# Reordering the first convolution steps and the second group's layer norm in a fused H3 + gated-MLP kernel

## The chip, the cores and the metric

The kernel runs on one core of one Trainium2 chip. The time is the device time of one execution in microseconds; the figure for a version is the median of its runs. A separate execution was recorded by the hardware profiler; its rows are what the durations below come from. In the profile PE is TensorE's matmul row, PEld its weight loads, DVE is VectorE, ACT is ScalarE, POOL is GpSimd and SP is SyncE, whose own instructions (SPq) issue nearly all DMAs of this kernel.

## The reference, cut to what matters

The input `x` (`A_q`) has 2048 rows of 640. Its rows are layer-normed to `xn`, and the output is `x` plus two branches of `xn`:

```python
xn = layernorm(x)                                   # per row, 640 wide
kv = shift_conv(k, shift_k) * v                     # 4 taps along the sequence
y  = irfft(rfft(kv, 4096) * rfft(ssm_k, 4096))[:2048]   # causal convolution by FFT
A  = xn * (y + kv * ssm_D)
B  = (sigmoid(xn @ w_gate) * (xn @ w_up)) @ w_down  # 640 -> 1728 -> 640
out = x + A + B
```

All data are bf16, with float32 accumulation.

## The kernel before, in words

**Layout.** Row `16p + b` of the sequence lies on partition `p`, block `b`; there are 16 blocks, handled as four groups of four (`g` or `t` in the code). The MLP works on one group (512 rows) at a time. The convolution works on five chunks of 128 channels (`c`), for all 2048 rows, as a discrete Fourier transform in stages: a first stage of matmuls against a cosine and sine table `S1t`, a write to DRAM and a read back in another arrangement, a second stage, the product with the kernel's transform, and two inverse stages.

**MLP.** For a group, each of 13 columns of 128 takes a gate product and an up product (`product`, L281, five matmuls of 512 columns into one PSUM tile), ScalarE's sigmoid (L290) and VectorE's multiplication into `hT` (L296); a last, narrower one is done in one go (L302, L308, L311). Then come eight down tiles (L325), each of two half-tiles of seven matmuls, evicted by VectorE, which adds them onto `x` (L330). All these PSUM tiles rotate through four buffers (`psG`). The products read `xnT`, the transposed `xn` of the group; it has one buffer. For the first group it is made by TensorE; for groups 1 to 3 by four DMA transposes (`xn_turn`, L260), one a block, called turns here.

**Layer norm of a group** (`ln_norms`, L210 and L214: statistics of a block; `ln_pow`, L222: GpSimd's power −1/2; `ln_xn`, L227: VectorE's subtraction and multiplication). For the second group alone (`g == 1`), two of its four blocks are normalised by ScalarE (`ln_xn_act`, L239), for which GpSimd first works out a bias (`ln_shift`, L233 and L234). Its input block of `x` is loaded by L135 in the middle of the table loads.

**Convolution.** VectorE makes `kv` (L358 to L367, sixteen instructions a chunk) and transposes the filter (L344); GpSimd adds `ssm_D` to it (L338). A first-stage step (`st1_mm`, L384 and L386) is eight matmuls into one of two PSUM buffers (`psC`), evicted by ScalarE (`st1_ev`, L242). A chunk has eight such steps; steps 0 to 3 read the first half of `S1t`, steps 4 to 7 the second. Two steps make a tile of 512 KB, which SyncE writes to DRAM (`wr1`, L402), four writes a chunk; `rd2` (L419) reads it back.

**Order.** Nothing is reordered by a scheduler. Every function call is a step of a chain named by a letter, and the string `ORDER` says from which chain the next step is taken; each engine runs its instructions in that order. The letters that matter here: `g` a product or a down half-tile on PE; `s` sigmoid; `u` VectorE's eviction of a product or down tile; `a` a first-stage step and `A` its eviction; `w` a write of it; `l` a block's statistics or its normalisation on VectorE; `P` the power on GpSimd; `x` the normalisation on ScalarE; `e` a turn; `k` one of `kv`'s instructions; `H` the filter's transposition, `D` the addition on GpSimd; `K` loads of `k`, `T` of the taps, `n` of later groups of `x`.

**SyncE's queue.** All DMAs but a few at the start are issued by SyncE, in the string's order. An instruction that waits there holds all those behind it. The build gives the queue eight semaphores in turn, so that a DMA also waits until the one eight places before it has landed.

The change lies in the second row of `ORDER`, where group 0's down tiles, the first-stage steps of chunk 0 (and the first ones of chunk 1) and the second group's layer norm meet, just ahead of the second group's products.

Of the kernel before, what the change touches and what calls it, by code (L numbers as in the profile page):

```python
# [11 lines left out]
F32 = mybir.dt.float32  # L12
U16 = mybir.dt.uint16
ACT = mybir.ActivationFunctionType
ALU = mybir.AluOpType
# [4 lines left out]
P = 128  # L20
# [37 lines left out]
def kernel(  # L58
# [14 lines left out]
    nc = tc.nc  # L73
# [15 lines left out]
    cv = ctx.enter_context(tc.tile_pool(name="cv", bufs=1))  # L89
# [16 lines left out]
    x = res.tile([P, NB, DM], BF16, name="x")  # L106
    xn = res.tile([P, NB, DM], BF16, name="xn")
# [93 lines left out]
    lns = [dict() for _ in range(4)]  # L201
# [22 lines left out]
    def ln_xn(g, i):  # L224
# [1 line left out]
        d = lns[g]  # L226
        nc.vector.tensor_scalar(xn[:, b, :], x[:, b, :], d["mv"][:, i, 0:1], d["rstd"][:, i:i + 1],  # L227
                                op0=ALU.subtract, op1=ALU.mult)

    def ln_shift(g, lo):  # L230
        d = lns[g]
        d["nb"] = cv.tile([P, 4], F32, name="nb")
        nc.gpsimd.tensor_tensor(d["nb"][:, lo:4], d["mv"][:, lo:4, 0], d["rstd"][:, lo:4], ALU.mult)  # L233
        nc.gpsimd.tensor_scalar(d["nb"][:, lo:4], d["nb"][:, lo:4], -1.0, None, op0=ALU.mult)  # L234

    def ln_xn_act(g, i):
        b = 4 * g + i
        d = lns[g]
        nc.scalar.activation(xn[:, b, :], x[:, b, :], ACT.Identity, bias=d["nb"][:, i:i + 1], scale=d["rstd"][:, i:i + 1])  # L239

    def act_copy(out, in_):
        nc.scalar.copy(out=out, in_=in_)  # L242
# [310 lines left out]
        up_ev(0, fc)  # L553


    chains = {k: [] for k in "ABCDHKPRTVWZabcdeghklmnopqrstuwx"}

    def step(k, fn, *args):
        chains[k].append((fn, args))
# [87 lines left out]
                    step(k, *a)  # L647

    for g in range(1, 4):
        for i in range(4):  # L650
            step("l", ln_norms, g, i)
        step("P", ln_pow, g, 0, 4)
        if g == 1:
            step("P", ln_shift, g, 2)
        for i in range(4):
            if g == 1 and i >= 2:
                step("x", ln_xn_act, g, i)
            else:
                step("l", ln_xn, g, i)
        for i in range(4):  # L660
            step("e", xn_turn, g, i)

# [8 lines left out]

    ORDER = """
    mmmZmmmmmmmmmTmmmmmmmggsguggsggsuukkgggssukkggukksukkkgsgukkgggsgukkkggsgsukkguHstggguHDmmmsukkkkggg
    ulagluaAKglulaAwAaAgPPukalAlkkHDkweegakkAxxeeTggakgggaAaAgKwaukgukAHukggAukkwsgggnustagukKKgghakAsul
    rwAsakggluglsaksAugHggkAVrubkkkBlswKBukgggaTVsgpkusukawgDkHPlngAaAaskgAKwAkukgskpbgtkBsllBugauAkgagp
    sAaguswVpakAguhkHHAgrgDkwcgVklguCkkraeCagAgkAbuBkuBkkggKgkbBKpggBaeualwukkggeIuurlTklAehrgwtVbBBggag
    kAagppswuAagkuaKswrgpAAkaHAskWgHupDgakuVsAggswucglJukkgkrCsbgpBugaBaAgAWkkgsbspugPkrBgwpgsRnFkukgprc
# [40 lines left out]
```

## Time and profile before

| | |
|---|---|
| Median of 3 runs | 234.88 us (233.32 to 235.01) |
| Profiled execution: device time | 236.44 us |
| Profiled execution: span from first to last instruction | 234.7 us |
| Mean granted TensorE clock | 0.999 |
| PE busy, idle | 227.9 us (97%), 6.8 us |
| DVE busy | 203.4 us (87%) |
| ACT busy | 123.4 us (53%) |
| DMA queue 1 (SyncE's and ScalarE's) | 56.03 MB, 93.4% of 16 engines' span |

The profiled execution's device time is 1.7 us more than its span, and 1.56 us more than the median of the runs. In the profile's rows a matmul's duration overlaps with the next one's; how fast PE goes is read from the distance of their starts. Rows of SPq are the issuing of a DMA and not its transfer; the trace also has the time at which most DMAs landed.

### The profile page before, as it was taken

What the parts mean: (1) busy time and instruction counts of PE and PEld (TensorE: products, weight loads), DVE (VectorE), ACT (ScalarE), POOL (GpSimd) and SP (SyncE); (2) the same over time, 40 slices, a digit from 0 to 9 for tenths busy, and PEclk for the clock granted to TensorE, in tenths of its full rate; (3) what the DMA queues carried; (4) which work ended last, traced back from release to release, by engine and by line L of the source; (5) the groups of instructions that cost most, each with busy time, mean ns of one, the idle gap of its engine ahead of it and who ended that gap; (6) DMA issues with size and microseconds to landing.
All of it is one profiled execution on the core that took longest, in us unless ns stands there. A gap on an engine that the chain in (4) does not pass through costs nothing.

```text
span 234.7 us, 5420 instructions
## 1 busy us (share of the span) xinstructions
PE 227.9 (97%) x2200; PEld 130.5 (56%) x2200; DVE 203.4 (87%) x357; ACT 123.4 (53%) x158; POOL 11.8 (5%) x25
## 2 busy tenths in 40 slices
PE   7899999889999999999999999999999999999995
PEld 2754446658454455677654534478754544436772
DVE  5446999399979999999999999997889999897774
ACT  2533222467446778576586747674556667762000
POOL 5210000021001100000011000000000000000000
PEclk9999999999999999999999999999999999999999
DMA  6999999978799989999979899579999998464774
GB/s 191 325 288 266 211 253 362 193 180 184 219 293 291 272 306 253 302 221 231 327 205 311 214 335 279 174 196 166 256 267 310 290 244 240 125 146 129 226 256 146
DMA packets 93803, 56.79 MB, mean 242 GB/s; under 512 B 50964, under 2 KB 87890, under 8 KB 93650
## 3 DMA queue, kind: packets, MB, share of 16 engines
q1 hardware_dynamic: 93346, 56.03, 93.4%
q10 hardware_dynamic: 432, 0.41, 0.5%
q8 instruction: 17, 0.28, 0.5%
q14 instruction: 8, 0.07, 0.1%
HBM read 36.12 MB, written 18.35 MB: 232 GB/s over the span
## 4 chain that ended last, share of the span: by engine, by line
PE 78%; DMA 11%; SPq 9%; issue 1%; DVE 0%
PE pd L325 23%; PE pu L281 18%; PE pg L281 18%; DMA S1t<-tabS 7%; PE psb L498 4%; PE ps L384 4%; PE ps L386 4%; DMA w<-in_B_w_up_dram 3%; PE ps L428 3%; PE psa L457 2%; SPq L187 2%; PE pg L302 1%; SPq L190 1%; SPq L183 1%; SPq L169 1%; DMA x<-in_A_q_dram 1%
## 5 line engine op out<-in xcount | busy, mean ns | idle before, releaser
L281 PEld LDWEIGHTS <-w 128*128 128x128 bf16 x500 | 46.6, 98 | 54.4 <-issue 4.9
L325 PE MATMUL pd<-wd,hT 128*128 128x320 bf16 (+2 forms) x448 | 66.0, 299 | 0.0
L281 PE MATMUL pg<-xnT,w 128*128 128x512 bf16 x250 | 62.2, 379 | 0.3 <-issue 0.3
L281 PE MATMUL pu<-xnT,w 128*128 128x512 bf16 x250 | 62.2, 379 | 0.0
L325 PEld LDWEIGHTS <-hT 128*128 128x128 bf16 x448 | 41.7, 98 | 18.2 <-issue 2.4
L290 ACT ACTIVATE sig<-pg 128x512 bf16<-128x512 f32 x52 | 31.1, 601 | 30.9 <-PE pg L281 29.1
L296 DVE TENSOR_TENSOR hT<-sig,pu 128x512 bf16<-128x512 bf16 x52 | 35.0, 680 | 10.7 <-PE pu L281 5.2
L242 ACT CAST xz<-ps 128x1024 bf16<-128x1024 f32 x36 | 35.1, 1014 | 15.8 <-PE ps L428 15.7
L242 ACT CAST t<-ps 128x1024 bf16<-128x1024 f32 x24 | 23.7, 1013 | 17.7 <-PE ps L386 14.6
L443 DVE TENSOR_TENSOR xz<-xz 128x2048 bf16<-128x2048 bf16 x20 | 24.4, 1221 | 0.2
L384 PE MATMUL ps<-kvh,S1t 128*128 128x128 bf16 x160 | 21.4, 218 | 1.8 <-DMA S1t<-tabS 1.8
L386 PE MATMUL ps<-kvh,S1t 128*128 128x128 bf16 x160 | 21.5, 220 | 0.0
L362 DVE TENSOR_TENSOR tmp<-kx,sc 128x1024 bf16<-128x1024 bf16 x30 | 20.5, 682 | 0.3
L364 DVE TENSOR_TENSOR acc<-acc,tmp 128x1024 bf16<-128x1024 bf16 x30 | 20.5, 682 | 0.3
L330 DVE TENSOR_TENSOR x<-pd,x 128x320 bf16<-128x320 f32 (+2 forms) x32 | 15.0, 476 | 3.9 <-PE pd L325 3.8
L384 PEld LDWEIGHTS <-S1t 128*128 128x128 bf16 x160 | 15.5, 97 | 4.9 <-DMA S1t<-tabS 2.5
L210 DVE BATCH_NORM_STATS2 st<-x 128x6 f32<-128x320 bf16 x32 | 13.9, 477 | 4.9 <-DMA x<-in_A_q_dram 4.9
L386 PEld LDWEIGHTS <-S1t 128*128 128x128 bf16 x160 | 15.4, 96 | 2.5
L242 ACT CAST TBt<-ps 128x1024 bf16<-128x1024 f32 x14 | 13.8, 1012 | 4.6 <-PE ps L386 4.6
L503 DVE TENSOR_TENSOR yx<-psb,xn 128x512 bf16<-128x512 f32 x20 | 13.7, 687 | 1.7 <-PE psb L498 0.8
L441 DVE STREAM_SHUFFLE xz<-xz 128x512 f32<-128x512 f32 x20 | 14.6, 728 | 0.0
L242 ACT CAST ao<-psa 128x1024 bf16<-128x1024 f32 x9 | 9.0, 1013 | 8.3 <-PE psa L457 8.2
(56 smaller groups left out, 158.2 us busy)
## 6 DMA issues: line engine op xcount, KB each, us to landing
t<-d SPq DMA_DIRECT2D x15, 512.0 KB, 6.0
d<-t SPq DMA_DIRECT2D x13, 512.0 KB, 5.5
d<-TBt SPq DMA_DIRECT2D x7, 512.0 KB, 6.3
d<-ao SPq DMA_DIRECT2D x6, 512.0 KB, 4.7
bi<-d SPq DMA_DIRECT2D x6, 512.0 KB, 4.8
kvh<-in_A_v_dram SPq DMA_DIRECT2D x10, 256.0 KB, 6.6
hn<-in_A_ssm_k_dram SPq DMA_DIRECT2D x20, 128.0 KB, 5.8
S1t<-d SPq DMA_DIRECT2D x4, 512.0 KB, 5.9
```

The lines of the kernel that those rows point to most:

```text
L242: nc.scalar.copy(out=out, in_=in_)
L281: nc.tensor.matmul(pg[:, :], lhsT=w[:, c, u * UP + fc * P:u * UP + (fc + 1) * P], rhs=xnT[:, :, c, :], start=(c == 0), stop=(c == NC - 1))
L290: nc.scalar.activation(sig[fc][:, :], pgs[0, fc][:, :], ACT.Sigmoid)
L296: nc.vector.tensor_tensor(hT[:, fc, :], sig[fc][:, :], pgs[1, fc][:, :], ALU.mult)
L325: nc.tensor.matmul(pd[:, :], lhsT=hT[:, fc, bb * P:(bb + 1) * P], rhs=wd[:, fc, es], start=(fc == 0), stop=(fc == NFC - 1))
L330: nc.vector.tensor_tensor(x[:, 4 * t + bb, es], pds[bb, half][:, :], x[:, 4 * t + bb, es], ALU.add)
L362: nc.vector.tensor_tensor(d["tmp"][:, :, :], kx[:, lo + 3 - m:hi + 3 - m, :], sb(m), ALU.mult)
L364: nc.vector.tensor_tensor(d["acc"][:, :, :], d["acc"][:, :, :], d["tmp"][:, :, :], ALU.add)
L384: nc.tensor.matmul(ps[:, i, 0:P], lhsT=S1[:, h, b, :], rhs=cin[c]["kvh"][:, 0, b, :], start=True, stop=True)
L386: nc.tensor.matmul(ps[:, i, P:2 * P], lhsT=S1[:, h, b, :], rhs=hp[:, b // 2, b % 2, :], start=True, stop=True)
L441: nc.vector.stream_shuffle(z[:, 2, :, :].bitcast(F32), z[:, 1, :, :].bitcast(F32), swap)
L443: nc.vector.tensor_tensor(z[:, 1:3, :, :], z[:, 0:1, :, :].to_broadcast((P, 2, 8, P)), z[:, 1:3, :, :], ALU.mult)
```

## The change

In the second row of `ORDER`: two more down half-tiles stand ahead of chunk 0's first `a`, and after it `g` and `a` alternate; two of `kv`'s instructions and an eviction stand ahead of the second group's first statistics; the power is taken for blocks 0 and 1 as soon as their statistics are there and then for blocks 2 and 3; VectorE normalises all four blocks; the first two turns stand ahead of the first two writes, the last two behind these and ahead of the loads (`K`, `T`) that stood ahead of all of them; further on one `w` stands ahead of a `K`, and in the row's tail one `g` and one `a` change places. The row's steps are otherwise the same, and all other rows are unchanged. GpSimd's bias and ScalarE's normalisation are gone.

```diff
-    def ln_shift(g, lo):
-        d = lns[g]
-        d["nb"] = cv.tile([P, 4], F32, name="nb")
-        nc.gpsimd.tensor_tensor(d["nb"][:, lo:4], d["mv"][:, lo:4, 0], d["rstd"][:, lo:4], ALU.mult)
-        nc.gpsimd.tensor_scalar(d["nb"][:, lo:4], d["nb"][:, lo:4], -1.0, None, op0=ALU.mult)
-
-    def ln_xn_act(g, i):
-        b = 4 * g + i
-        d = lns[g]
-        nc.scalar.activation(xn[:, b, :], x[:, b, :], ACT.Identity, bias=d["nb"][:, i:i + 1], scale=d["rstd"][:, i:i + 1])
-
...
     for g in range(1, 4):
-        for i in range(4):
-            step("l", ln_norms, g, i)
-        step("P", ln_pow, g, 0, 4)
-        if g == 1:
-            step("P", ln_shift, g, 2)
-        for i in range(4):
-            if g == 1 and i >= 2:
-                step("x", ln_xn_act, g, i)
-            else:
-                step("l", ln_xn, g, i)
+        for lo, hi in (((0, 2), (2, 4)) if g == 1 else ((0, 4),)):
+            for i in range(lo, hi):
+                step("l", ln_norms, g, i)
+                if g == 1 and i == 2:
+                    step("l", ln_xn, g, 0)
+                    step("l", ln_xn, g, 1)
+            step("P", ln_pow, g, lo, hi)
+        for i in range(2 if g == 1 else 0, 4):
+            step("l", ln_xn, g, i)
         for i in range(4):
             step("e", xn_turn, g, i)
...
-    ulagluaAKglulaAwAaAgPPukalAlkkHDkweegakkAxxeeTggakgggaAaAgKwaukgukAHukggAukkwsgggnustagukKKgghakAsul
+    ukgukgaAlugaAlPgaAlllueewgaAwlPgaAklleeHDkgaAugaAkKTwgaAukkKwgaAukkHgaAukkkggsgggnustgaukKKgghakAsul
```

## The prediction

> **What bounds the kernel now.** First the page's head and slices:
>
> ```profile
> span 234.7 us, 5420 instructions
> PE 227.9 (97%) x2200; PEld 130.5 (56%) x2200; DVE 203.4 (87%) x357; ACT 123.4 (53%) x158; POOL 11.8 (5%) x25
> PE   7899999889999999999999999999999999999995
> DVE  5446999399979999999999999997889999897774
> DMA  6999999978799989999979899579999998464774
> ```
>
> PE hardly idles. A product of five 512-column matmuls advances it by 1.08 us, so these rows are PE at its pace, and time is won only where PE waits. Its timeline has three waits between the fill and the tail, all in the stretch the change rewrites:
>
> ```profile
> 43.04 0.23 PE L384 MATMUL ps<-kvh,S1t 128*128 128x128 bf16 x1 [0.70 <-DMA S1t<-tabS]
> ...
> 48.99 0.23 PE L384 MATMUL ps<-kvh,S1t 128*128 128x128 bf16 x1 [1.11 <-DMA S1t<-tabS]
> ...
> 59.80 1.24 PE L281 MATMUL pg<-xnT,w 128*128 128x512 bf16 x5 [0.31 <-issue]
> ```
>
> Two are for the halves of S1t. The third is the second group's first product; "issue" names nothing, so I look at what it reads: SyncE's timeline.
>
> ```profile
> 45.81 4.16 SPq L165 DMA_DIRECT2D kx<-in_A_k_dram  x1
> 50.01 0.49 SPq L166 DMA_DIRECT2D kx<-in_A_k_dram  x1
> 50.60 0.82 SPq L402 DMA_DIRECT2D d<-t  x2
> 52.45 5.90 SPq L260 DMA_TRANSPOSE xnT<-xn  x4
> 58.40 0.57 SPq L149 DMA_DIRECT2D sraw<-in_A_shift_k_dram  x1
> 59.03 0.42 SPq L161 DMA_DIRECT2D kx<-in_A_k_dram  x1
> 59.49 1.05 SPq L402 DMA_DIRECT2D d<-TBt  x2
> 60.59 1.07 SPq L135 DMA_DIRECT2D x<-in_A_q_dram  x1
> ```
>
> The four turns hold SyncE for 1.94, 1.22, 1.23 and 1.23 us. The first three landed at 56.60, 57.27 and 58.41; the fourth's landing is not in the trace, but the one before landed 1.4 us after its issuing ended, and 58.35 + 1.4 = 59.75 is when PE goes on. **The third wait is for the last turn.** Last, VectorE:
>
> ```profile
> 45.82 0.89 DVE L210 BATCH_NORM_STATS2 st<-x 128x6 f32<-128x320 bf16 x2 [2.95 <-DMA x<-in_A_q_dram]
> 51.94 0.80 DVE L227 TENSOR_SCALAR xn<-x,mv,rstd 128x640 bf16<-128x640 bf16 x2 [0.26 <-POOL rstd L222]
> ...
> 67.44 0.69 DVE L296 TENSOR_TENSOR hT<-sig,pu 128x512 bf16<-128x512 bf16 x1 [1.16 <-ACT sig L290]
> ```
>
> It waits for x's second group (landed 45.79), then for the power, then at 67.44 for PE's product; after 0.24 us at 71.08 it has no gap over 0.15 us until 135.46. From 71 to 135 VectorE is as full as PE.
>
> **PE, part by part.** A half-tile advances PE by 0.95 us (three from 53.22 to 56.07), a first-stage step by 0.46. The last half-tile before the row begins at 41.22, so PE is free at 42.17. From there to 59.80 it runs 11 half-tiles (10.45) and 10 steps (4.6), 15.05 in all: without waits it would be at the product at 57.22. The waits cost 2.58 by this count (0.87, 1.28 and 0.43; the rows show 0.70, 1.11 and 0.31, since modelled ends overlap).
>
> With two half-tiles ahead, step 0 comes at 42.17 + 1.90 = 44.07, and its half of S1t is there by 43.04: cover 1.03. Step 4 comes after six half-tiles and four steps, 49.71; the second half landed at 48.94: cover 0.77. Both transfers are issued before the changed row, so they don't move. **The first two waits go, 2.15 us.** Steps now come 1.41 apart, and ScalarE's eviction takes 1.01 of that. Late next could be step 8, chunk 1's first, at 55.35: it needs VectorE's last `kv` product (54.9 by the walk below) and GpSimd's addition (55.1): cover 0.25, and a miss would fall inside the wait that follows.
>
> **VectorE.** Two of `kv`'s instructions and an eviction (0.72 + 0.61 + 0.34 by distance of starts) move into the 2.95 us gap and cost nothing there. Two more normalisations cost 0.36 each. By distances of the rows (statistics of a block 1.06, an eviction 0.34) the walk from 45.82 gives: block 0, eviction, blocks 1 and 2, then normalisation of 0 and 1 from 49.33 to 50.14; eviction, block 3 until 51.48, a `kv` addition, normalisation of 2 and 3 from 52.35 to 53.2. The power of two columns is not in the trace: one takes 0.55 to 0.57, four take 1.02. I take 0.72; with 1.02 the first pair would start at 49.5. GpSimd's 0.20 + 0.22 for the bias and ScalarE's two 0.91 go, with no one behind them on the path. So turns can start at **49.8 instead of 52.45**. VectorE comes to the second group's first multiplication at 62.4 (63.46 before), in time for a PE that comes to it after 59 us.
>
> **SyncE decides what follows.** Turn 0 stands where the halo load L165 stood; that one was held until 49.97, and the turn behind the same transfers gets 1.4 us (1.2 alone, 1.94 at most by the first row above). Turn 1 ends at 52.5, and the writes are issued at 52.6 and 53.1. **Turns 2 and 3 are still behind both writes, 1 MB.** In the trace a turn right behind DMA ends its issuing 2.07 us after one write (102.22 to 104.29), 3.34 after the second of these very writes (51.05 to 54.39), 4.37 after a read and a write (153.15 to 157.52, where the turn took 3.78). I take 3.34, the same writes: turn 2 ends at 56.4, turn 3 another 1.33 later at 57.75 instead of 58.35, and lands at 59.2 (57.8 to 60.4 by the other two rows).
>
> So PE, ready at 57.22, starts the product at about 59.25 instead of 59.80. **The two waits for S1t are turned into one of 2 us for the last turn; 0.55 us is left.**
>
> At this place the Trainium skill speaks for more: "Advanced Engine Details and Errata", section "X-Bar Transpose (TRN2)", has transpose DMAs as fast as regular ones. Here a plain 512 KB write in this stretch holds SyncE for 0.36 to 0.58 us and a turn of 160 KB for 1.2 to 3.78, so the trace does not agree as to the issuing; by the page (an estimate, with 0.4 us a turn as for a write) the last turn would be issued by 54 us, and this would be rival B.
>
> **Does the rest keep it?** Behind turn 3 SyncE has the two halo loads (1.0 us), taps, `k` load and two writes (2.1) before the load of x's third group: issued at 57.75 + 3.1 = 60.85, against 60.59 before. Queue 1 is nearly idle at 59 to 61 (0.04 and 0.06 MB each us), so the landing, 67.75 before, follows the issue: 68.0. VectorE's statistics of it began at 68.05, so VectorE is not earlier from there on; it can drop its 0.24 us wait at 71.08. PE, 0.55 earlier, then meets buffers that VectorE frees: the tightest start 0.36 (at 92.26) and 0.34 us (at 143.50) after the eviction. 0.24 + 0.34 = 0.58 is allowed, 0.55 needed. The DRAM reads land 1.1 us or more ahead of PE's use all through, and nearly all 2 us or more, so they follow. The swap in the tail moves a step of 0.46 behind a product and changes no sum.
>
> Sum: 2.15 (S1t) + 0.43 (last turn) − 2.03 (the new wait) = 0.55. On the profiled execution's 236.44 that is 235.9; it lies 1.56 above the median, so the median becomes 234.88 − 0.55, or **234.3**.
>
> **Rivals.**
> A (this forecast), the last turn is late by about as much as before; result between 1.3 faster and 0.3 slower. Chance 0.5.
>
> B, the writes don't hold the turns: each takes 1.22, turn 3 ends at 56.0, lands at 57.4. PE gains 2.4; x's third group lands 1.5 earlier or more, and VectorE allows about 2.1 to 2.3. 232.7. For it: 1.2 us is the commonest row; against it: all three rows of turns behind transfers. The skill's rule above, worked out as here, is this case. Chance 0.25 (1.3 to 2.6 faster).
>
> C, slower: turns 2 and 3 take as long as the longest rows behind transfers, 3.78 and 3.03 us. Then turn 3 ends at about 60.8 and lands at 62.3, PE's product is 2.5 late; the load of x's third group goes out 3.3 late, and VectorE is 3 late, less 0.58 of slack. 234.88 + 2.4 = 237.3. The point from which it decides: turn 3's issuing ends after 58.35. For it: group 3's turns; against it: the queue there also carried reads back from DRAM. Chance 0.25 (0.3 to 2.5 slower).
>
> That the change does nothing but move the waits is A itself.
>
> **How the numbers follow.** The likeliest case gives 234.3. The runs before spread over 1.69 us, so a shift under 1% (2.35 us) can hardly be told from none. The range leaves out the ends of B and C and takes in 0.8 of spread around the rest: 232.4 to 236.4. Faster by over 1% is half of B and a little spread, 0.15; slower by over 1% is under half of C, 0.12; within it, 0.73.
>
> **What would show it.** PE without a wait at chunk 0's first-stage steps; one wait of about 2 us ahead of the first product of the second group, at about 59.2; the first turn issued near 49.8, the third at 53.5 held for 2 us or more behind two writes; the load of x's third group issued near 60.9; VectorE's first third-group statistics near 68. It is wrong if the turns behind the writes hold SyncE for 1.2 us only (B) or well over 3 (C), or if step 8 is what PE waits for.

## The result and the profile after

The changed kernel takes 235.29 us in the median of nine runs (234.96 to 235.78); nine runs of the kernel before, beside them, take 234.15 (233.23 to 237.32). The ratio is 1.0054, with a 95% interval of 1.0031 to 1.0076: slower by half a per cent. Ratios, here and below, leave out runs more than 1.5% above the fastest of their kernel, here the one of 237.32. That is inside the range and inside the 1% that was called "the same", but the forecast was a gain of 0.55 us and it became a loss.

The profiled execution of the changed kernel took 235.41 us, 1.03 *less* than the 236.44 of the one before. The page's head and slices:

```profile
span 233.6 us, 5418 instructions
PE 228.1 (98%) x2199; PEld 130.9 (56%) x2200; DVE 203.8 (87%) x359; ACT 122.0 (52%) x156; POOL 12.0 (5%) x24
PE   7999999998999999999999999999999999999995
DVE  5446999889679999999999999997899999897773
DMA  6999999999899899999999899589989999464874
```

VectorE has two instructions more and ScalarE two fewer. Of PE's two 8s between 41 and 53 us one is left, from 53 to 58, and VectorE's slice with a 3, from 41 to 47, has an 8. PE's timeline (start, duration, line, operation, in brackets the idle time before it and what ended it; from `L249` on, lines of the changed kernel are 11 lower than before):

```profile
43.86 0.22 PE L373 MATMUL ps<-kvh,S1t 128*128 128x128 bf16 x1
...
49.47 0.22 PE L373 MATMUL ps<-kvh,S1t 128*128 128x128 bf16 x1
...
58.22 1.24 PE L270 MATMUL pg<-xnT,w 128*128 128x512 bf16 x5 [1.12 <-DMA xnT<-xn]
...
123.72 1.24 PE L270 MATMUL pu<-xnT,w 128*128 128x512 bf16 x5 [0.27 <-DVE hT L285]
```

Steps 0 and 4 have no wait any more. The first product of the second group waits 1.12 us for a turn, and starts at 58.22. A wait for VectorE at 123.72 is new. SyncE's timeline (start, how long the issuing held the queue):

```profile
48.17 3.64 SPq L249 DMA_TRANSPOSE xnT<-xn  x2
51.91 1.00 SPq L391 DMA_DIRECT2D d<-t  x2
53.00 3.65 SPq L249 DMA_TRANSPOSE xnT<-xn  x2
56.70 0.57 SPq L165 DMA_DIRECT2D kx<-in_A_k_dram  x1
57.32 0.47 SPq L166 DMA_DIRECT2D kx<-in_A_k_dram  x1
57.84 0.38 SPq L149 DMA_DIRECT2D sraw<-in_A_shift_k_dram  x1
58.32 0.37 SPq L391 DMA_DIRECT2D d<-TBt  x1
58.74 0.43 SPq L161 DMA_DIRECT2D kx<-in_A_k_dram  x1
59.27 1.08 SPq L391 DMA_DIRECT2D d<-TBt  x1
60.40 0.49 SPq L135 DMA_DIRECT2D x<-in_A_q_dram  x1
```

Two turns, two writes, two turns: the turns were issued in 1.31, 2.21, 2.31 and 1.24 us and landed at 53.05, 53.52, 57.38 and 58.09. The halo loads (L165, L166) are now behind them, and the load of x's third group is issued at 60.40. VectorE where that block arrives:

```profile
62.81 0.69 DVE L285 TENSOR_TENSOR hT<-sig,pu 128x512 bf16<-128x512 bf16 x1 [0.96 <-ACT sc L157]
64.55 0.69 DVE L347 TENSOR_TENSOR acc<-kx,sc 128x1024 bf16<-128x1024 bf16 x1 [1.06 <-DMA kx<-in_A_k_dram]
...
66.94 0.69 DVE L285 TENSOR_TENSOR hT<-sig,pu 128x512 bf16<-128x512 bf16 x1 [1.09 <-ACT sig L279]
67.79 0.89 DVE L210 BATCH_NORM_STATS2 st<-x 128x6 f32<-128x320 bf16 x2 [0.16 <-DMA x<-in_A_q_dram]
...
68.85 0.63 DVE L353 TENSOR_TENSOR acc<-acc,tmp 128x1024 bf16<-128x1024 bf16 x1
```

It waits at 62.81 for ScalarE, at 64.55 for a load of `k`, at 66.94 for the third sigmoid of the group and at 67.79, shortly, for the block of `x`. So far this is the forecast's picture: no S1t waits, one wait for the last turn, statistics at 67.79 where 68.0 was forecast. The profile even gains 1.03 us. Yet the medians lose 1.14. The two profiled executions therefore can't be compared as they stand, and the experiments begin there. Three causes of the loss were to be told apart: that the S1t waits belong to that one execution and the gain was never there; that the new wait for the last turn costs more than it replaced; and that something later, on VectorE, is set back.

### The profile page after: what moved, and what is told of

The parts are those of the page before. It is cut to its first block, busy times and chain, and to the rows that moved or that the text cites. A ratio compares the mean times of both kernels' runs of the same rounds, so it can differ in the third digit from the quotient of the medians.

```text
span 233.6 us, 5418 instructions
## 1 busy us (share of the span) xinstructions
PE 228.1 (98%) x2199; PEld 130.9 (56%) x2200; DVE 203.8 (87%) x359; ACT 122.0 (52%) x156; POOL 12.0 (5%) x24
## 4 chain that ended last, share of the span: by engine, by line
PE 91%; DVE 6%; DMA 1%; POOL 0%; issue 0%; ACT 0%; DVEq 0%
PE pu L270 24%; PE pg L270 23%; PE pd L314 22%; PE psb L487 4%; PE ps L417 3%; PE ps L375 3%; PE ps L373 3%; PE psa L446 2%; PE idle L513 2%; PE pg L291 2%; DVE st L210 1%; DVE x L319 1%; DMA xnT<-xn 1%; PE pg L261 1%; PE pu L261 1%; PE pt L241 1%
```

## The experiments

The diffs show the string of the second row; a time ratio is to the kernel before on the same chip. From comparison to comparison the median of the kernel before lay between 234.15 and 235.71 us, so ratios and not medians are compared.

### Both kernels once more, unchanged

> The kernel before once more, unchanged, with another profile. Theory 1 (the profiled execution was not a usual one: its loads between 33 and 49 us landed late, and the waits for S1t are mostly its own): the second half of S1t lands at 46 to 47 us, not at 48.9; the waits for S1t and for the last turn sum to under 1 us instead of 2.1; the span is about 232.4. Theory 2 (the waits are there in every execution, and the change loses its gain further on): waits of 1.7 to 2.1 us again, span 234 or more.

> The kernel before a third time, for its profile on the same chip. If the execution of the prediction was an unusual one: S1t's second half landed by 46.9, at most 0.3 us of waits at the first-stage steps, the second group's first product within 0.6 us of 57.7, a span of 232.0 to 233.0. If late loads are usual: landed after 48, waits of 1.5 or more, span over 234.

> The changed kernel once more, unchanged. If its loss has the causes found: a wait of 0.8 to 1.4 us ahead of the second group's first product, VectorE's statistics of the third group held until 67.5 to 68, a span of 233.3 to 233.9, and slower than before by 0.2 to 0.8% on this chip too.

The kernel before came out at 234.22 (0.9983, 0.9944 to 1.0023) and 234.03 (0.999), the changed one at 235.51 (1.0035, 0.9996 to 1.0073). The repetition points the same way as the first comparison, but its interval takes in 1. More telling are the traces. One more execution of the kernel before, span 232.56 and time 234.35, page and PE timeline:

```profile
span 232.6 us, 5420 instructions
PE   7999999999999999999999999999999999999995
```

```profile
42.19 0.22 PE L384 MATMUL ps<-kvh,S1t 128*128 128x128 bf16 x1
...
46.85 0.22 PE L384 MATMUL ps<-kvh,S1t 128*128 128x128 bf16 x1
...
57.72 1.24 PE L281 MATMUL pg<-xnT,w 128*128 128x512 bf16 x5 [0.28 <-issue]
```

**The S1t waits are not there.** The loads are issued at the same places (x's second group at 32.02 and S1t's second half at 32.52, against 32.44 and 32.91 in the profile the forecast used), but land at 44.32 and 46.37, where that profile had 45.79 and 48.94. All that is left for the change to win here is 0.28 us. In the third trace of the same kernel (span 234.09) x lands at 45.82 and S1t at 47.76, again without a wait for S1t, and the product starts at 59.25; there PE lost 0.84 us at 38.12 to a load of the down weights, ahead of the changed row. So an execution can be late without the waits that the change is aimed at. Of 138 runs of the kernel before, over all comparisons, a quarter lie under 233.84, the median is 234.99, and 24 are at 236.4 or over: the execution that the forecast was worked out from is of the slowest fifth.

The fast end is where the kernels differ. In the two comparisons in which both ran, one of 21 runs of the changed kernel is under 234.9, and 25 of 43 of the kernel before. At the slow end they don't: 5 of these 21 runs of the changed kernel are at 236.4 or over.

SyncE and VectorE in this execution of the kernel before, to be read against the rows of the changed kernel above:

```profile
50.98 5.30 SPq L260 DMA_TRANSPOSE xnT<-xn  x4
56.33 0.57 SPq L149 DMA_DIRECT2D sraw<-in_A_shift_k_dram  x1
56.95 0.42 SPq L161 DMA_DIRECT2D kx<-in_A_k_dram  x1
57.42 1.06 SPq L402 DMA_DIRECT2D d<-TBt  x2
58.53 1.05 SPq L135 DMA_DIRECT2D x<-in_A_q_dram  x1
```

```profile
65.36 0.69 DVE L296 TENSOR_TENSOR hT<-sig,pu 128x512 bf16<-128x512 bf16 x1 [0.89 <-ACT sig L290]
65.96 0.88 DVE L210 BATCH_NORM_STATS2 st<-x 128x6 f32<-128x320 bf16 x2
...
67.08 0.63 DVE L364 TENSOR_TENSOR acc<-acc,tmp 128x1024 bf16<-128x1024 bf16 x1
```

The changed kernel is 0.50 us later at the gate (58.22 against 57.72; "the gate" is from here on the first product of the second group), but 1.77 later on VectorE (68.85 against 67.08). Its load of x's third group is issued 1.87 later. The second trace of the changed kernel (span 233.29) has the gate at 58.24 and the addition at 68.61; there the block of `x` landed at 67.07, ahead of its use, and the sigmoid alone made VectorE late.

**What VectorE's delay costs.** The product at 129.18 in the changed kernel (the up product of the third group's sixth column) is followed by the same 104.4 to 104.7 us in all traces, so all differences lie ahead of it. In the three traces of the kernel before it comes 70.38 after the gate each time: PE's own pace. In the changed kernel PE comes to VectorE's row at 123.72 too early and waits. The `kv` addition at 68.85 plus 60.2 gives 129.07. I read the product's start as the later of *gate + 70.38* and *addition + 60.22* (the 60.22 is fitted on the traces where VectorE is late). For the execution just shown these are 128.10 and 127.30: VectorE has **0.80 us of cover**: it could be so much later before PE would have to wait. For the changed kernel they are 128.60 and 129.07: PE is 0.50 later, and VectorE, which had 0.80 of cover, now sets the product 0.47 later still. The sum, 0.97, stands against 1.08 in the rows (128.10 to 129.18), 1.06 in the spans and 1.14 in the medians. Over all 18 traces the rule is within 0.11 us in 13; the five others are 0.35, 0.41, 0.86, 0.92 and 2.07 later than it says, so it is a description and not a proof.

### The parts alone

*Steps two half-tiles later*, on the kernel before; layer norm, turns and loads keep their order on each queue:

```diff
-ulagluaAKglulaAwAaAgPPukalAlkkHDkweegakkAxxeeTggakgggaAaAgKwaukgukAHukggAukkwsgggnustagukKKgghakAsul
+ulglugaAKlulgaAwgaAPPukgaAllkkHDkweegaAkkgaAxxeeTkgaAgaAKwukgaAukHgaAukggukkwsgggnustagukKKgghakAsul
```

> Only the first-stage steps two half-tiles later; layer norm, ScalarE's share, turns, writes and loads in the order of before. Theory 1: little to win, as the waits are small in a usual execution: 0.5 faster to 0.2 slower than before. Theory 2: 1.3 to 2.1 faster up to the second group's products, of which 0.5 or more is left at the end.

Ratio 0.9992 (0.9955 to 1.0029), span 232.62, gate at 57.78: the kernel before, to 0.06 us. The trace has no wait for S1t, but neither has the kernel before in an execution with loads as early as here (S1t at 46.51). The part which was to bring 2.15 us brings nothing that can be measured.

*Power in pairs and VectorE's normalisation alone*, on the changed kernel's code with all else where it was before:

```diff
-ukgukgaAlugaAlPgaAlllueewgaAwlPgaAklleeHDkgaAugaAkKTwgaAukkKwgaAukkHgaAukkkggsgggnustgaukKKgghakAsul
+ulagluPaAKgluaAwAaAgllulPkaAllkkHDkweegakkAeeTggakgggaAaAgKwaukgukAHukggAukkwsgggnustagukKKgghakAsul
```

> Only the layer norm's part: the power in two pairs and VectorE alone; steps, turns, writes and loads in the places of before. Theory 1: VectorE's two more normalisations and the second power's wait make it 0.2 to 0.8 slower than before. Theory 2: within 0.2 of before.

Ratio 1.0013 (0.998 to 1.0047), span 232.69, gate at 57.51. The two added normalisations cost nothing that can be measured, as forecast.

*The swap in the row's tail alone*, on the kernel before:

```diff
-...wsgggnustagukKKgghakAsul
+...wsgggnustgaukKKgghakAsul
```

> The kernel before with one pair changed in the row's tail, as the change has it: the up product stands ahead of chunk 1's third first-stage step, not behind it. Theory S (the swap delays VectorE: ScalarE's eviction of that step stands ahead of the next sigmoid in its order and now ends 1.08 us later, and VectorE's multiplication waits for that sigmoid): the multiplication near 65.4 in the usual execution of before comes near 66.4, VectorE is 0.8 to 1.1 late from there to 133 us, PE 0.4 to 0.7 late from about 123, span 233.0 to 233.3 where the usual one has 232.6. Rival (the swap changes no sum, as the prediction had it): span within 0.15 of 232.6.

Ratio 0.9993 (0.9952 to 1.0034). The span, 231.99, is below what was expected, because this execution's loads were early (x at 42.89, gate at 56.86). But the mechanism is in the rows. VectorE and, ahead of it, ScalarE, and then ScalarE in the execution of the kernel before shown above:

```profile
65.57 0.69 DVE L296 TENSOR_TENSOR hT<-sig,pu 128x512 bf16<-128x512 bf16 x1 [2.24 <-ACT sig L290]
```

```profile
64.03 1.01 ACT L242 CAST t<-ps 128x1024 bf16<-128x1024 f32 x1 [2.60 <-issue]
64.94 0.60 ACT L290 ACTIVATE sig<-pg 128x512 bf16<-128x512 f32 x1
```

```profile
63.81 1.01 ACT L242 CAST t<-ps 128x1024 bf16<-128x1024 f32 x1 [1.50 <-issue]
64.72 0.60 ACT L290 ACTIVATE sig<-pg 128x512 bf16<-128x512 f32 x1
```

The sigmoid stands behind the step's eviction on ScalarE, and the step is now one product later. From gate to sigmoid it is 8.08 us here, as in the changed kernel (58.22 to 66.30), and 7.00 in all three traces of the kernel before: 1.08, one product. That uses up VectorE's cover of 0.80 and, by the rule above, costs 0.28: 56.86 + 70.38 = 127.24 against 67.30 + 60.22 = 127.52, and the product starts at 127.52. In the median such a size can't be seen, and it isn't.

### Undoing parts of the change

*All four turns ahead of the writes:*

```diff
-ukgukgaAlugaAlPgaAlllueewgaAwlPgaAklleeHDkgaAug...
+ukgukgaAlugaAlPgaAlllueegaAlPgaAklleewwHDkgaAug...
```

> The changed kernel with all four turns ahead of the first two writes. Theory 1, with the writes as what holds the last turns: the wait of 1.12 us ahead of the second group's first product shrinks under 0.3, and the time falls from 235.3 to 234.2 to 234.8. Theory 2 (VectorE, or the load of x's third group, decides later): the wait goes too, but the time stays within 0.3 of 235.3.

The last turn lands at 56.10 instead of 58.09 and PE's wait at the gate is gone (57.44). The time stays: 1.004 (1.0 to 1.008), span 233.40. VectorE shows why:

```profile
64.79 0.69 DVE L347 TENSOR_TENSOR acc<-kx,sc 128x1024 bf16<-128x1024 bf16 x1 [1.83 <-DMA kx<-in_A_k_dram]
...
67.67 0.89 DVE L210 BATCH_NORM_STATS2 st<-x 128x6 f32<-128x320 bf16 x2 [0.83 <-DMA x<-in_A_q_dram]
```

The third group's block, issued at 60.67, lands at 67.65, and VectorE is as late as in the changed kernel. So the new wait at the gate is not by itself what costs the time. The writes do hold the turns: the third turn took 2.16 to 2.31 us in the seven traces in which it stands right behind the two writes, and 1.21 in the four in which it stands ahead of them.

*The tail swapped back*, in the changed kernel (two runs):

```diff
-...gaAukkkggsgggnustgaukKKgghakAsul
+...gaAukkkggsgggnustagukKKgghakAsul
```

> The changed kernel with only that pair put back. Theory S with the load of x's third group as a second cause in the same place: the multiplication comes 1.08 earlier, near 65.9, but VectorE then waits for x's third group until 67.7 as before; span within 0.25 of the changed kernel's 233.6. If the swap alone decides: 0.5 to 0.8 us shorter.

> The changed kernel with the tail's pair put back, again, as the profile of the first one fell into an execution with late loads. With loads as usual: product at 58.2, VectorE's multiplication behind the sigmoid 1.0 us earlier than in the changed kernel (65.9), then VectorE at the mercy of x's third group (landed 67 to 67.8); span 233.0 to 233.5 (changed kernel 233.3 and 233.6).

Ratios 1.0053 (1.0017 to 1.0089) and 1.0003 (0.997 to 1.0036). The first trace has a granted clock of 0.993 and late loads (x's second group at 45.67, gate at 59.53), so its later rows can't be compared with the others. In the second the sigmoid comes 7.00 after the gate again, at 65.27, and VectorE's third multiplication at 66.46 instead of 66.94. Then:

```profile
68.76 0.89 DVE L210 BATCH_NORM_STATS2 st<-x 128x6 f32<-128x320 bf16 x2 [1.62 <-DMA x<-in_A_q_dram]
```

The load holds VectorE instead. It was issued at 60.47, as in the changed kernel, but landed at 68.73, 0.97 later, and the span is 234.71 where 233.0 to 233.5 was expected.

*The first halo loads at the row's start*, where they stand early as in the kernel before, and the same with the tail swapped back:

```diff
-ukgukgaAlugaAlPgaAlllueewgaAwlPgaAklleeHDkgaAugaAkKTwgaAukkK...
+KukgukgaAlugaAlPgaAlllueewgaAwlPgaAklleeHDkgaAugaAkTwgaAukkK...
```

> The changed kernel with one step moved: the two halo loads of k (L165, L166) stand ahead of everything in the row, where SyncE otherwise waits from 42.7 to 48.2 us for the first normalised block. Theory 1a (the load order behind the turns is what the change costs): taps, k load and the load of x's third group are issued about 1.1 us earlier than in the changed kernel (the last near 59.3, not 60.4) and land 0.8 to 1.3 earlier; VectorE's waits for them, 0.96 + 1.06 + 0.16, shrink by about 1; the time falls by 0.4 to 0.9 against the changed kernel. Rival 1b (the writes ahead of the last two turns are the cost): the wait ahead of the second group's first product stays near 1.1 and the time stays within 0.2.

> The changed kernel with the halo loads first and the tail's pair put back, and nothing else. If these two moves (SyncE's queue and the sigmoid) are the whole loss: product near 57.8, multiplication near 65.4, x's third group landed by 66.6, VectorE within 0.5 us of the usual kernel before at 69 us, span within 0.3 of 232.6. If VectorE's two more normalisations or the second power cost in themselves: 233 or more.

1.0037 (0.9992 to 1.0083) and 1.0034 (0.9992 to 1.0077): not settled. In the first trace the third group's block lands 1.2 us earlier, at 66.54, ahead of its use, and now it is the sigmoid (65.86) that VectorE waits for; span 232.81:

```profile
66.50 0.69 DVE L285 TENSOR_TENSOR hT<-sig,pu 128x512 bf16<-128x512 bf16 x1 [1.80 <-ACT sig L279]
```

The second has late loads (x at 44.88) and a wait of 2.19 at the gate, by the times for the last turn behind the writes (its issuing ended at 58.18; the gate is at 59.65); span 234.47.

*Halo loads early and all four turns ahead of the writes*, without and with the tail swapped back (the second shown against the changed kernel):

```diff
-ukgukgaAlugaAlPgaAlllueewgaAwlPgaAklleeHDkgaAugaAkKTwgaAukkKwgaAukkHgaAukkkggsgggnustgaukKKgghakAsul
+KukgukgaAlugaAlPgaAlllueegaAlPgaAklleewwHDkgaAugaAkTKgaAukkwwgaAukkHgaAukkkggsgggnustagukKKgghakAsul
```

> The halo loads first, all four turns ahead of the first two writes, and taps and k load ahead of the third and fourth write as in the kernel before. Theory 1a: no wait ahead of the second group's first product, VectorE's waits for loads gone, the load of x's third group issued near 58.3; equal to the kernel before or up to 0.6 us faster, 0.8 to 1.6 faster than the changed kernel. Rival (VectorE's two more normalisations or the second power cost in themselves): 0.3 to 0.8 slower than before still.

> As that, with all four turns ahead of the first writes and taps and k load ahead of the third and fourth. Product near 57.0, multiplication near 64.7; x's third group then holds VectorE until 66 to 66.5. Span 231.8 to 232.4, up to 0.7 us shorter than the usual kernel before; in time no more than 0.3% faster, which the runs may not tell.

Without the swap back 1.0013 (0.997 to 1.0055), span 232.25. With it **233.71 us, 0.9975 (0.9939 to 1.001)**, nine of ten runs between 233.48 and 233.96. Its interval lies under the changed kernel's 1.0031 to 1.0076 of the first comparison (and overlaps with that of the repetition, 0.9996 to 1.0073); no change from the kernel before is inside it. PE's, SyncE's and VectorE's rows:

```profile
56.72 1.24 PE L270 MATMUL pg<-xnT,w 128*128 128x512 bf16 x5
```

```profile
44.26 3.54 SPq L165 DMA_DIRECT2D kx<-in_A_k_dram  x1
47.85 0.49 SPq L166 DMA_DIRECT2D kx<-in_A_k_dram  x1
48.51 5.88 SPq L249 DMA_TRANSPOSE xnT<-xn  x4
54.48 1.00 SPq L391 DMA_DIRECT2D d<-t  x2
...
59.06 0.89 SPq L135 DMA_DIRECT2D x<-in_A_q_dram  x1
```

```profile
65.79 0.89 DVE L210 BATCH_NORM_STATS2 st<-x 128x6 f32<-128x320 bf16 x2 [0.75 <-DMA x<-in_A_q_dram]
...
66.85 0.63 DVE L353 TENSOR_TENSOR acc<-acc,tmp 128x1024 bf16<-128x1024 bf16 x1
```

No wait at the gate, which comes 1.50 earlier than in the changed kernel, the third group's load issued 1.34 earlier, VectorE's addition 2.00 earlier. Chunk 0's halo loads occupy SyncE while it would wait for the first normalisation anyway: the first turn starts at 48.51 against 48.17.

*The same with the load of x's third group right behind the first two writes:*

```diff
-...gaAklleewwHDkgaAugaAkTKgaAukkwwgaAukkHgaAukkkggsgggnustagukKKgghakAsul
+...gaAklleewwnHDkgaAugaAkTKgaAukkwwgaAukkHgaAukkkggsgggustagukKKgghakAsul
```

> Halo loads first, all turns ahead of the first writes, the pair put back, and the load of x's third group right behind those writes: no wait ahead of the second group's first product (57.0), the multiplication near 64.8, x's third group landed by 63, no wait of VectorE for a load; span 231.7 to 232.3, 0.3 to 0.8 us shorter than the usual one of before and 1.3 to 1.9 shorter than the changed kernel's. If VectorE's own two more normalisations cost: 232.5 or more.

1.0021 (0.9983 to 1.006): a miss. Its trace (span 236.26, x's second group at 45.85) has the gate at 58.35 with a wait of 0.98, where 57.0 and none was expected, and PE waits 0.94 at 76.37 for the read of the second stage. That the early load pushes this read back is a guess that no run tests.

### Late loads on purpose

The same addition to both kernels: one more load of a later group's block of `x` (640 KB) ahead of S1t's first half, a piece of work that isn't in either kernel; the block is loaded again at its normal place. The added `m` in the first row of the string is the step of this load.

```diff
+              (load_x, sync, 3),
               (sync.dma_start, S1t[:, 0, :, :], S1d.ap()[:, 0, :, :]),
...
-    mmmZmmmmmmmmmTmmmmmmmggsg...
+    mmmZmmmmmmmmmTmmmmmmmmggsg...
```

> The kernel before with one more load of 640 KB (x's fourth group, loaded again later) ahead of S1t, so that S1t and all loads behind it land late, as they did in the execution that the prediction was worked out from. Theory 1: the second half of S1t lands at 48 to 49 instead of 46.4, PE waits for it 1.0 to 1.7 us and for the first half up to 0.9, and the time is 1.2 to 2.2 longer than before's. Theory 2 (that execution was slow for another reason): under 0.5 longer.

> The changed kernel with the same added load. Theory 1: PE has no wait at the first-stage steps, but everything behind the second group of x is as late, so the wait for the last turn grows by 0.5 to 1.7; 0.8 to 2.0 longer than the changed kernel, and against the late kernel before from 0.6 faster to 0.4 slower, so the change's loss of about 1.1 shrinks or turns. Theory 2: the loss of 1.1 stays.

S1t's halves land at 45.09 and 50.14 in the kernel before and at 43.57 and 48.16 in the changed one. PE's waits, before and then changed:

```profile
45.13 0.23 PE L384 MATMUL ps<-kvh,S1t 128*128 128x128 bf16 x1 [1.85 <-DMA S1t<-tabS]
50.18 0.23 PE L384 MATMUL ps<-kvh,S1t 128*128 128x128 bf16 x1 [0.21 <-DMA S1t<-tabS]
...
61.97 1.24 PE L281 MATMUL pg<-xnT,w 128*128 128x512 bf16 x5 [0.51 <-DVE x L330]
```

```profile
59.07 1.25 PE L270 MATMUL pg<-xnT,w 128*128 128x512 bf16 x5 [1.34 <-DMA xnT<-xn]
81.09 1.24 PE L270 MATMUL pu<-xnT,w 128*128 128x512 bf16 x5 [0.68 <-DVE hT L285]
```

The waits for S1t are there, 1.85 for the first half and 0.21 for the second, the other way round than expected. The changed kernel's profile is 1.38 us *shorter* (span 235.37 against 236.75), and the medians, 237.03 of twelve runs (changed) and 237.93 of six (before), stand the other way round than without the load, though the ratios' intervals (1.006, 1.0016 to 1.0104, and 1.010, 1.003 to 1.017) overlap. The two traces are not alike in their loads, however: the changed kernel's landed 1.52 and 1.98 us earlier. Its step 0 stands at 44.00, so with the landing of the other trace, 45.09, it would have waited too, 1.09 us, and step 4 would then have come after the second half. So the waits that the change is aimed at exist with late loads; at such landings the order would remove about 1.0 of their 2.06 us, which is an estimate from these rows and not a measurement.

## Why the prediction was wrong

**The step that failed is "The first two waits go, 2.15 us", taken off the median.** The waits go, that is right: steps 0 and 4 run without one, the working by distances (0.95 and 0.46 us) placed them to 0.3 us, and in the order of the changed kernel step 4 has no wait even where the second half landed at 47.96 to 48.16 (three traces, step 4 at 49.56 to 49.62). But the 2.15 was a property of one execution, whose S1t landed 2.6 us later than in another of the same program. The text saw that this execution lay 1.56 above the median, and then subtracted the whole gain from the median. In the kernel's faster executions there is nothing to remove: 0.28 ahead of the gate. Set against its own execution the forecast seems to hold, with −0.55 forecast and −1.03 measured (236.44 to 235.41), but that is luck: in the changed kernel's execution x's second group landed 1.73 us earlier and S1t's second half 2.68.

**SyncE and the gate: the mechanism held, sizes off by about 1 us.** The first turn was issued at 48.17 (49.8 forecast, with x landing 1.7 earlier) and the third at 53.00 (53.5). From the start of the second write to the end of the third turn's issuing it took 2.77 us, not 3.34: the rows that 3.34 was read from have 1.03 us in them (51.42 to 52.45) in which SyncE waited for the normalised block and not for the writes. PE was ready at 57.10 (57.22 forecast), and the wait at the gate was 1.12, not 2.03. With early loads it is a floor: with x's second group landing anywhere from 42.0 to 44.1 the gate of three executions is at 58.22, 58.24 and 58.27, and the last turn lands at 58.09 to 58.14, wherever the first was issued (47.90 to 48.63). The kernel before has no such floor in these traces: its gate is at 57.72, 59.25 and 59.80 with x at 44.32, 45.82 and 45.79, and, in the trace with the tail's swap alone, which lies behind the gate, at 56.86 with x at 42.89. So the change loses against the executions with early loads. That it wins in those with late ones isn't shown: with x at 45.67 the gate in the changed order came at 59.53 (at a clock of 0.993), between the 59.25 and 59.80 of the kernel before.

**"The swap in the tail … changes no sum" was wrong.** It counted PE alone. The eviction behind that step stands ahead of a sigmoid on ScalarE, which VectorE waits for: 1.08 us, more than VectorE's cover of 0.80.

**"Does the rest keep it?" asked the wrong question.** The landing was forecast well (issued 60.85, landing 68.0; 60.40 and 67.76), and compared with 67.75 of the late execution. In the execution shown above it is issued at 58.53 and lands at 65.58. The changed kernel moves the halo loads behind the turns, and SyncE, which issues nothing from 42.71 to 48.17, pays for them later, ahead of the load. Either delay on VectorE is enough by itself: with the wait at the gate gone the load holds it, with the swap undone the load holds it, with the load earlier the sigmoid holds it. By these traces that is why single undoings won little, and the fastest version is the one that undoes all three. That these delays together make the loss is shown as far as that version takes it back; what each is worth in time isn't.

**Power and normalisation: right.** The power of two columns took 0.70 and 1.02 us (0.72 taken, 1.02 named), and the part alone costs nothing measurable.

**The rivals.** B is out: the third turn took 2.31 behind the writes and 1.21 with the writes put behind it, and the last landed at 58.09 instead of 57.4. The Trainium skill's rule ("Advanced Engine Details and Errata", section "X-Bar Transpose (TRN2)"), by which a transposing DMA would be as fast as a regular one, doesn't agree with the issuing here either: 1.21 us at least for a turn, 0.5 for a write of three times its size (two in 1.00). C did not come either: turn 3's issuing ended at 56.65, ahead of its point of decision at 58.35. The loss came by a way no rival had: VectorE, set back by other steps of the same row.

**What stays open.** Why the same loads land 2 to 3 us apart between executions; how the loss divides between gate, sigmoid and load in time and not only in traces, since single runs of these kernels differ by more than the parts do; and whether the fastest version beats the kernel before, which its interval leaves undecided.

## What to carry to other kernels

Before a wait in a profile is priced, look where that execution stands among the runs: a wait on a load in an execution above the median may not be there in the usual ones, and its removal is worth its share of the executions, not its length. When a transfer is moved behind others in an in-order queue, follow the whole queue to the next load that a nearly full engine needs. A step moved by one product on the engine that is full moves its eviction, and with it whatever stands behind that eviction on a quieter engine.

## What the runs showed of the hardware

- Loads issued at the same points of the program landed at different times: S1t's second half at 46.37, 47.76 and 48.94 us in three executions of one kernel, issued at 32.52 to 32.95.
- A DMA transpose of 160 KB held SyncE 1.2 to 1.3 us in most cases, but in the changed order the first of a row took 1.30 to 2.33 and the second 1.21 to 2.67, with no write between or right ahead of them, and the third 2.16 to 2.31 right behind two writes of 512 KB against 1.21 without them.
- A halo load, small as it is, held SyncE for 3.54 to 4.16 us behind the table and `v` loads (L165's row at 44.26, 44.34 and 45.81), and 0.57 us at 56.70, behind the turns. In its early place it cost the turns little: the first was issued at 48.51 with the halo loads ahead of it and at 48.17 without, since SyncE would have waited there for the first normalised block.
